# Linear attention feeding an MLP: attention matmuls on 64-column tiles, and the last token block in column pieces

## Chip, cores, metric

The kernel runs on one core of a Trainium2 chip (trn2). The metric is the device time of one execution in microseconds. A ratio is the mean time of one kernel's fast runs over that of the other's in the same rounds, so it is not quite the ratio of the medians that are quoted beside it.

## The reference

Blocked linear attention with decay (4 sequences, 8 heads, 768 positions, head size 64), then an MLP of 512 -> 2048 -> 512 with a sigmoid-approximated GELU over all 3072 tokens. Cut to what matters:

```python
for b in range(nb):                                    # blocks of 64 positions
    intra = (qb @ kb.T * Dmask) @ vb
    inter = (qb * lam_pow) @ kv_state
    out[:, :, sl] = intra + inter
    kv_state = lam_block * kv_state + (kb * rev_pow).T @ vb
...
h = x @ w_in                                           # x: [3072, 512]
return (h * sigmoid(1.702 * h)) @ w_out
```

## The kernel before

The kernel works on six token blocks of 512 tokens. The first two are "double blocks" (256 positions of two sequences, written with `d_...`); the other four are "single blocks" (128 positions of four sequences, `n_...`). Each attention part is slipped in between the MLP matmuls of the token block before it. Two heads share the 128 partitions as a pair `r` or `p`. For the matmul that gives `v.T @ scores` the weights are 128 columns wide, one head's 64 columns of `v` beside 64 zero columns: each head's matmul then adds zeros to the other head's half. The state matmul takes both heads' `k` columns against both heads' `v` columns, and only the two diagonal quarters of its result are used.

```python
v_sb = [const.tile([P, B, NP, 3, D], bf16, ...) for i in range(2)]     # v of head 0 | zeros | v of head 1

def d_state(w, c):                                     # state of a double block
    ...
    for r in range(NP):
        for a in range(2):
            nc.tensor.matmul(one[:, r, :], ks[A, a, r*P:(r+1)*P], vt[A, 2*c+a, r, 0:3:2, :], ...)
    ...                                                # the same with all 128 rows into `two`
def n_state(w, p):                                     # state of a single block, head pair p
    for b in range(B):
        nc.tensor.matmul(ps_kv[:, b, :], cast[...,"k"][:, b%2, p*P:(p+1)*P], v_sb[w%2][:, b, p, 0:3:2, :], ...)
    ...
def n_out(w, p):                                       # output of a single block, head pair p
    for b in range(B):
        nc.tensor.matmul(ps_o[:, b, :], kv[:, b, p, :], qT[:, (b%2)*NP + p, :], start=True, stop=False)
        for h in range(2):
            nc.tensor.matmul(ps_o[:, b, :], vt[:, b, p, h:h+2, :]..., masked[w, p, h][:, b, :], ...)
    ...
# the order in which single-block parts are slipped in; t counts groups of four MLP matmuls
side += [(t, (n_two, x, 0)), (t + 2, (n_two, x, 1))]                    # scores and masks
if x + 1 < NW:
    side += [(t + 2*p + 1, (n_state, x, p)) for p in range(NP)]
side += [(t + 4.5 + 2*p, (n_out, x, p)) for p in range(NP)]
```

The end of the program is the last group of 128 tokens: 16 matmuls into a 128x512 accumulator, one copy out of PSUM by VectorE, one store.

Of the kernel before, what the change touches and what calls it, by code (L numbers as in the profile page):

```python
# [24 lines left out]
def kernel(  # L25
# [13 lines left out]
    nc = tc.nc  # L39
    f32 = mybir.dt.float32  # L40
    bf16 = mybir.dt.bfloat16
    B, H, S, D = q.shape
    P = 128
    NP = H // 2
    W = 512
    ND = 2
    G = W // P
    d_model = H * D
# [9 lines left out]
    MUL = mybir.AluOpType.mult  # L58
    ADD = mybir.AluOpType.add

    NW = S // P

    const = ctx.enter_context(tc.tile_pool(name="const", bufs=1))
# [4 lines left out]
    op = ctx.enter_context(tc.tile_pool(name="op", bufs=4))  # L68
    ps = ctx.enter_context(tc.tile_pool(name="ps", bufs=1, space=bass.MemoryType.PSUM))
# [35 lines left out]
    A, Z = slice(0, 64), slice(64, P)  # L105
# [45 lines left out]
    mk_pow(blk_pow, 1.0 * P)  # L151
    warm = const.tile([P, 1], f32)

    v_sb = [const.tile([P, B, NP, 3, D], bf16, name=f"v_sb{i}") for i in range(2)]
    kv_sb = [const.tile([P, B, NP, P], bf16, name=f"kv{i}") for i in range(2)]

    CW = 4
    NCH = FFC // CW
    w_in_sb = [const.tile([P, KC, CW * P], bf16, name=f"w_in{j}") for j in range(NCH)]
    w_out_sb = [const.tile([P, CW, d_model], bf16, name=f"w_out{j}") for j in range(NCH)]  # L160
# [12 lines left out]
    cast, trans, masked, xT, g_of, h_ps, o_ps, t_ps = {}, {}, {}, {}, {}, {}, {}, {}  # L173

    def acc(name, dt=f32, shape=None):
        return ps.tile(shape or [P, 4, P], dt, tag="a", bufs=5, name=name)
# [15 lines left out]
    def cast_v(w, c):  # L192
        f = loaded.pop((w, c, "v"))
        dst = v_sb[w % 2]
        if w < ND:
            for a in range(2):
                nc.gpsimd.tensor_copy(dst[:, 2 * c + a, :, 0:3:2, :],  # L197
                                      f.rearrange("p (r e) (a d) -> p r e a d", e=2, a=2)[:, :, :, a, :])
        else:
            nc.gpsimd.tensor_copy(dst[:, 2 * c : 2 * c + 2, :, 0:3:2, :].rearrange("p b r e d -> p (b r) e d"),  # L200
                                  f.rearrange("p h (a d) -> p h a d", a=2))

    def turn_pe(w, c, nm):
        x = cast[w, c, nm]
# [34 lines left out]

    def d_state(w, c):  # L240
        ks, vt, b = cast[w, c, "k"], v_sb[w % 2], 2 * w + c
        one, two = acc("ps_kv"), acc("ps_kv")
        for r in range(NP):
            for a in range(2):
                nc.tensor.matmul(one[:, r, :], ks[A, a, r * P : (r + 1) * P], vt[A, 2 * c + a, r, 0:3:2, :],  # L245
                                 start=(a == 0), stop=(a == 1))
        for r in range(NP):
            for a in range(2):
                nc.tensor.matmul(two[:, r, :], ks[:, a, r * P : (r + 1) * P], vt[:, 2 * c + a, r, 0:3:2, :],
                                 start=(a == 0), stop=(a == 1))  # L250
        for i, t in ((1, one), (0, two)):
            for hs in (A, Z):
                nc.scalar.copy(kv_sb[i][hs, b, :, hs], t[hs, :, hs])  # L253

    def d_out(w, c):
        qT, vt, b = trans[w, c, "q"].rearrange("p (r t) s -> p r (t s)", r=NP), v_sb[w % 2], 2 * w + c
        oa, oz = acc("ps_o"), acc("ps_o")
        for r in range(NP):
            nc.tensor.matmul(oz[:, r, :], kv_sb[1][:, b, r, :], qT[:, r, P:], start=(r == 0), stop=False,
                             skip_group_check=True)  # L260
        for r in range(NP):
            for a in range(2):
                for h in range(2):
                    for t, bs in ((oa, A), (oz, Z)):
                        nc.tensor.matmul(t[:, r, :], vt[bs, 2 * c + a, r, h : h + 2, :].rearrange("p e d -> p (e d)"),  # L265
                                         masked[w, c, r // 2, h][bs, r % 2, a, :],
                                         start=(t is oa and r + a + h == 0), stop=(a + h == 2), skip_group_check=True)
        if w not in xT:
            xT[w] = xp.tile([P, NP, W], bf16, tag="x", name="xT")
        for i, t in ((0, oa), (1, oz)):  # L270
            n0 = (2 * c + i) * P
            nc.scalar.copy(xT[w][:, :, n0 : n0 + P], t)  # L272
# [21 lines left out]
                f(w, p)  # L294

    def n_state(w, p):
        ps_kv = acc("ps_kv")
        for b in range(B):
            nc.tensor.matmul(ps_kv[:, b, :], cast[w, b // 2, "k"][:, b % 2, p * P : (p + 1) * P],  # L299
                             v_sb[w % 2][:, b, p, 0:3:2, :], start=True, stop=True)  # L300
        new, old = kv_sb[(w + 1) % 2], kv_sb[w % 2]
        for h, hs in enumerate((A, Z)):
            nc.vector.scalar_tensor_tensor(new[hs, :, p, hs], old[hs, :, p, hs],  # L303
                                           blk_pow[hs, 2 * p + h : 2 * p + h + 1],
                                           ps_kv[hs, :, hs], op0=MUL, op1=ADD)

    def n_out(w, p):
        vt, kv = v_sb[w % 2], kv_sb[w % 2]
        ps_o = acc("ps_o")
        for b in range(B):  # L310
            qT = trans[w, b // 2, "q"]
            nc.tensor.matmul(ps_o[:, b, :], kv[:, b, p, :], qT[:, (b % 2) * NP + p, :], start=True, stop=False)  # L312
            for h in range(2):
                nc.tensor.matmul(ps_o[:, b, :], vt[:, b, p, h : h + 2, :].rearrange("p e d -> p (e d)"),  # L314
                                 masked[w, p, h][:, b, :], start=False, stop=(h == 1))
        if w not in xT:
            xT[w] = xp.tile([P, NP, W], bf16, tag="x", name="xT")
        nc.scalar.copy(xT[w][:, p, :], ps_o.rearrange("p b s -> p (b s)"))  # L318
# [11 lines left out]
        if h_ps[fc][1] == KC * W:  # L330
            nc.scalar.activation(g_of[w][:, fc, :], h_ps.pop(fc)[0], GELU)  # L331

    def mlp2(w, g, j):
        if j == 0:
            o_ps[w, g] = ps.tile([P, d_model], f32, tag="mm", bufs=3, name="ps_out")
        ps_out = o_ps[w, g]
        for fc in range(j * CW, (j + 1) * CW):
            nc.tensor.matmul(ps_out, g_of[w][:, fc, g * P : (g + 1) * P], w_out_sb[j][:, fc % CW, :],  # L338
                             start=(fc == 0), stop=(fc == FFC - 1))
        if j == NCH - 1:  # L340
            o = op.tile([P, d_model], f32, tag="o", name="o_sb")
            nc.vector.tensor_copy(o, ps_out)  # L342
            r0 = (2 * w + g // 2) * S + (g % 2) * P if w < ND else g * S + w * P
            nc.sync.dma_start(out=out[r0 : r0 + P, :], in_=o)

    EARLY = 3
    ALL = slice(0, W)
# [2 lines left out]
    def mlp_items(w):  # L350
        if w < ND:
            parts = [(full, slice(0, W // 2)), (full, slice(W // 2, W))]
        else:
            parts = [(full[:-1], ALL), (full[-1:], ALL)]
        first = [(mlp1, w, fc, kcs, cols) for kcs, cols in parts for fc in range(EARLY)]
        second = [(mlp1, w, fc, full, ALL) for fc in range(EARLY, FFC)]
        if w == 0:
            third = [(mlp2, w, g, j) for j in range(NCH) for g in range(2)]
            third += [(mlp2, w, g, j) for g in range(2, G) for j in range(NCH)]
        else:  # L360
            third = [(mlp2, w, g, j) for g in range(G) for j in range(NCH)]
        return first + second + third

    def gate_pool(x):
# [4 lines left out]

    with tc.manual_schedule():  # L370
        u32 = mybir.dt.uint32
        nc.vector.memset(v_sb[0][:, :, :, 1, :].bitcast(u32), 0)
        for x in kv_sb:
            nc.vector.memset(x.rearrange("p b r s -> p (b r s)").bitcast(u32), 0)
        nc.vector.memset(v_sb[1][:, :, :, 1, :].bitcast(u32), 0)
        nc.scalar.activation(warm, sd_pow[:, 0:1], GELU)

        do_cast(0, 0, "k", nc.vector)
        do_cast(0, 0, "q", nc.vector)
        cast_v(0, 0)  # L380
        do_cast(0, 1, "k", nc.gpsimd)
        gate_pool(loaded[0, 1, "q"][0:1, 0, 0:1])
# [6 lines left out]
        turn_pe(0, 1, "k")  # L389
        turn_pe(0, 1, "q")  # L390
        d_state(0, 0)
        d_out(0, 0)
        cast_v(0, 1)
        for j in range(1, NCH):
            load_w_in(j)
# [4 lines left out]
        d_scores(0, 1, 0)  # L400
        d_scores(0, 1, 1)
        d_state(0, 1)

        side, main = [(EARLY, (d_out, 0, 1))], []
        for w in range(NW):
            n = len(main)
            main += mlp_items(w)
            e = len(main)
            x = w + 1
            if x < ND:  # L410
                for c in range(HF):
                    t = e - 12 + 6 * c
# [5 lines left out]
            elif x < NW:  # L418
# [4 lines left out]
                t = n + 16  # L423
# [42 lines left out]
```

## Time and profile before

| | |
|---|---|
| time | 228.92 us median of 3 runs |
| span of the profiled execution | 226.8 us |
| TensorE (PE) busy | 205.9 us, 91% |
| MLP matmuls' share of the chain that ended last | 35% + 34% |

The page of the kernel before, cut: busy time and share of each engine; busy tenths in 40 slices; the chain of waits that ended last, by engine and then by line.

```profile
PE 205.9 (91%) x1536; PEld 110.6 (49%) x1560; DVE 92.6 (41%) x139; ACT 89.1 (39%) x157; POOL 24.6 (11%) x44
PE   0379799988999999999999999999999999999992
...
PE 82%; ACT 5%; DVE 4%; issue 3%; DMA 3%; SPq 0%; DVEq 0%
PE ps_out L338 35%; PE ps_h L327 34%; PE ps_o L314 3%; DMA qf<-in_q_dram 3%; PE ps_o L265 2%; DVE sm L287 2%; ACT xT L272 2%; ACT qT L213 2%; PE ps_o L312 2%; PE ps_s L280 1%; PE ps_t L208 1%; ACT g_sb L331 1%; DVE qs L183 1%; PE ps_s L231 1%; PE ps_kv L299 1%
```

TensorE is the limit from about 28 us, the sixth slice, on, so what counts is when it *starts* its next matmul. Its busy time is of little use for that, because matmuls overlap. The groups view names the attention matmuls (line, weights' rows*columns, moving shape, count, then busy us and mean ns of one):

```profile
L314 PE MATMUL ps_o<-sm,v_sb 128*128 128x128 bf16 x128 | 12.4, 219 | 0.0
L312 PE MATMUL ps_o<-qT,kv 128*128 128x128 bf16 x64 | 11.5, 219 | 0.0
L265 PE MATMUL ps_o<-sm,v_sb 64*128 64x128 bf16 x128 | 5.0, 238 | 0.0
L299 PE MATMUL ps_kv<-v_sb,ks 128*128 128x128 bf16 x48 | 4.6, 219 | 0.0
```

Each takes 219 to 238 ns from start to modelled end, but the timeline shows how often they start. Its columns are start in us, length of the merged piece, engine, line, operation and shapes, count. Two stretches of the third single block: a state part alone, and an output part followed by a state part.

```profile
108.79 0.39 PE L299 MATMUL ps_kv<-v_sb,ks 128*128 128x128 bf16 x4
109.02 1.03 PE L327 MATMUL ps_h<-xT,w_in 128*128 128x512 bf16 x4
109.98 0.45 PE L280 MATMUL ps_s<-qT,kT 64*128 64x128 bf16 x9
110.58 0.38 PE L280 MATMUL ps_s<-qT,kT 64*128 64x128 bf16 x7 [0.15 <-DVE sm L287]
110.89 1.04 PE L327 MATMUL ps_h<-xT,w_in 128*128 128x512 bf16 x4
...
113.71 0.22 PE L312 MATMUL ps_o<-qT,kv 128*128 128x128 bf16 x1
...
114.38 0.39 PE L299 MATMUL ps_kv<-v_sb,ks 128*128 128x128 bf16 x4
```

The next start is the thing to read: four state matmuls hold TensorE from 108.79 to 109.02, 56 ns each, and twelve output matmuls from 113.71 to 114.38, again 56 ns each.

### The profile page before, as it was taken

What the parts mean: (1) busy time and instruction counts of PE and PEld (TensorE: products, weight loads), DVE (VectorE), ACT (ScalarE), POOL (GpSimd) and SP (SyncE); (2) the same over time, 40 slices, a digit from 0 to 9 for tenths busy, and PEclk for the clock granted to TensorE, in tenths of its full rate; (3) what the DMA queues carried; (4) which work ended last, traced back from release to release, by engine and by line L of the source; (5) the groups of instructions that cost most, each with busy time, mean ns of one, the idle gap of its engine ahead of it and who ended that gap; (6) DMA issues with size and microseconds to landing.
All of it is one profiled execution on the core that took longest, in us unless ns stands there. A gap on an engine that the chain in (4) does not pass through costs nothing.

```text
span 226.8 us, 3726 instructions
## 1 busy us (share of the span) xinstructions
PE 205.9 (91%) x1536; PEld 110.6 (49%) x1560; DVE 92.6 (41%) x139; ACT 89.1 (39%) x157; POOL 24.6 (11%) x44
## 2 busy tenths in 40 slices
PE   0379799988999999999999999999999999999992
PEld 0257644545664465444465444565444564444440
DVE  4473200484780881280971371961452712100121
ACT  5635567246267422056322066322076321276000
POOL 4297000220120003000003000003000000000000
PEclk9999999999999999999999999999999999999998
DMA  5989999999999993169993189991292011200121
GB/s 144 291 169 206 198 200 267 289 248 213 244 242 203 206 225 99 46 141 201 206 227 110 47 172 200 222 219 68 77 155 51 0 49 60 79 0 3 46 80 59
DMA packets 86756, 33.79 MB, mean 149 GB/s; under 512 B 67284, under 2 KB 83668, under 8 KB 86740
## 3 DMA queue, kind: packets, MB, share of 16 engines
q1 hardware_dynamic: 82516, 29.37, 58.8%
q0 software_dynamic: 4224, 4.19, 11.5%
q8 instruction: 12, 0.20, 0.4%
q14 instruction: 4, 0.03, 0.0%
HBM read 27.27 MB, written 6.29 MB: 148 GB/s over the span
## 4 chain that ended last, share of the span: by engine, by line
PE 82%; ACT 5%; DVE 4%; issue 3%; DMA 3%; SPq 0%; DVEq 0%
PE ps_out L338 35%; PE ps_h L327 34%; PE ps_o L314 3%; DMA qf<-in_q_dram 3%; PE ps_o L265 2%; DVE sm L287 2%; ACT xT L272 2%; ACT qT L213 2%; PE ps_o L312 2%; PE ps_s L280 1%; PE ps_t L208 1%; ACT g_sb L331 1%; DVE qs L183 1%; PE ps_s L231 1%; PE ps_kv L299 1%
## 5 line engine op out<-in xcount | busy, mean ns | idle before, releaser
L327 PE MATMUL ps_h<-xT,w_in 128*128 128x512 bf16 (+1 forms) x397 | 86.2, 366 | 2.9 <-ACT xT L272 1.3
L338 PE MATMUL ps_out<-w_out,g_sb 128*128 128x512 bf16 x371 | 86.3, 379 | 0.9 <-issue 0.3
L331 ACT ACTIVATE g_sb<-ps_h 128x512 bf16<-128x512 f32 x96 | 56.0, 597 | 62.3 <-PE ps_h L327 61.8
L327 PEld LDWEIGHTS <-w_in 128*128 128x128 bf16 x408 | 39.0, 98 | 44.3 <-issue 3.6
L338 PEld LDWEIGHTS <-g_sb 128*128 128x128 bf16 x384 | 36.2, 98 | 38.8
L342 DVE COPY o_sb<-ps_out 128x512 f32<-128x512 f32 x24 | 16.6, 691 | 72.9 <-PE ps_out L338 72.9
L287 DVE SCALAR_TENSOR_TENSOR sm<-ps_s,inv_pow,mask 128x512 bf16<-128x512 f32 x32 | 21.7, 744 | 27.0 <-PE ps_s L280 26.9
L318 ACT CAST xT<-ps_o 128x512 bf16<-128x512 f32 x16 | 9.4, 586 | 30.9 <-PE ps_o L314 30.9
L200 POOL CAST v_sb<-vf 128x1024 bf16<-128x1024 f32 x8 | 9.0, 1123 | 96.6 <-DMA vf<-in_v_dram 96.6
L237 DVE SCALAR_TENSOR_TENSOR sm<-ps_s,sd_pow,mask_d 128x256 bf16<-128x256 f32 x32 | 13.1, 478 | 9.4 <-PE ps_s L231 9.4
L314 PE MATMUL ps_o<-sm,v_sb 128*128 128x128 bf16 x128 | 12.4, 219 | 0.0
L303 DVE SCALAR_TENSOR_TENSOR kv<-kv,blk_pow,ps_kv 64x256 bf16<-64x256 bf16 x24 | 11.5, 478 | 1.1 <-PE ps_kv L299 0.6
L312 PE MATMUL ps_o<-qT,kv 128*128 128x128 bf16 x64 | 11.5, 219 | 0.0
L183 DVE TENSOR_TENSOR ks<-kf,kd_pow 128x1024 bf16<-128x1024 f32 x3 | 3.7, 1223 | 17.6 <-DMA kf<-in_k_dram 16.0
L314 PEld LDWEIGHTS <-v_sb 128*128 128x128 bf16 x128 | 9.8, 98 | 1.9
L187 DVE TENSOR_TENSOR ks<-kf,k_pow 128x1024 bf16<-128x1024 f32 x8 | 10.7, 1336 | 0.1
L208 PE MATMUL ps_t<-ident,ks 128*128 128x128 bf16 x32 | 3.3, 265 | 7.9 <-DVE ks L183 7.1
L187 DVE TENSOR_TENSOR qs<-qf,q_pow 128x1024 bf16<-128x1024 f32 x8 | 9.7, 1218 | 0.0
L253 ACT CAST kv<-ps_kv 64x256 bf16<-64x256 f32 x16 | 5.9, 366 | 7.6 <-PE ps_kv L245 7.4
L197 POOL CAST v_sb<-vf 128x512 bf16<-128x512 f32 x8 | 4.8, 617 | 33.1 <-DMA vf<-in_v_dram 33.1
L211 ACT COPY kT<-ps_t 128x1024 bf16<-128x1024 bf16 x4 | 4.1, 1016 | 8.1 <-PE ps_t L208 8.1
L312 PEld LDWEIGHTS <-kv 128*128 128x128 bf16 x64 | 6.3, 98 | 1.9
(54 smaller groups left out, 88.5 us busy)
## 6 DMA issues: line engine op xcount, KB each, us to landing
kf<-in_k_dram SPq DMA_DIRECT2D x12, 512.0 KB, 6.8
qf<-in_q_dram SPq DMA_DIRECT2D x12, 512.0 KB, 7.5
vf<-in_v_dram SPq DMA_DIRECT2D x12, 512.0 KB, 7.3
out_dram<-o_sb SPq DMA_DIRECT2D x24, 256.0 KB, 2.0
w_in<-in_moe_w_in_dram POOLq DMA_DIRECT2D x4, 512.0 KB, 7.0
w_out<-in_moe_w_out_dram POOLq DMA_DIRECT2D x4, 512.0 KB, 15.0
kT<-ks SPq DMA_TRANSPOSE x8, 3.3
qT<-qs SPq DMA_TRANSPOSE x8, 3.3
```

The costliest lines, as they stand in the source:

```text
L187: eng.tensor_tensor(x.rearrange("p b (h d) -> p b h d", h=H), f.rearrange("p (b h) (a d) -> p b (h a) d", b=2, a=2), pw.unsqueeze(3).to_br ...
L200: nc.gpsimd.tensor_copy(dst[:, 2 * c : 2 * c + 2, :, 0:3:2, :].rearrange("p b r e d -> p (b r) e d"), f.rearrange("p h (a d) -> p h a d", ...
L237: nc.vector.scalar_tensor_tensor(sm[:, i], s2[h][:, i], sd_pow[:, hd : hd + 1], mask_d, op0=MUL, op1=MUL)
L287: nc.vector.scalar_tensor_tensor(sm, s, inv_pow[:, 2 * p + h : 2 * p + h + 1], mask.to_broadcast([P, B, P]), op0=MUL, op1=MUL)
L303: nc.vector.scalar_tensor_tensor(new[hs, :, p, hs], old[hs, :, p, hs], blk_pow[hs, 2 * p + h : 2 * p + h + 1], ps_kv[hs, :, hs], op0=MUL, ...
L312: nc.tensor.matmul(ps_o[:, b, :], kv[:, b, p, :], qT[:, (b % 2) * NP + p, :], start=True, stop=False)
L314: nc.tensor.matmul(ps_o[:, b, :], vt[:, b, p, h : h + 2, :].rearrange("p e d -> p (e d)"), masked[w, p, h][:, b, :], start=False, stop=(h ...
L318: nc.scalar.copy(xT[w][:, p, :], ps_o.rearrange("p b s -> p (b s)"))
L327: nc.tensor.matmul(h_ps[fc][0][:, cols], w_in_sb[j][:, kc, i * P : (i + 1) * P], xT[w][:, kc, cols], start=(kc == 0), stop=(kc == KC - 1))
L331: nc.scalar.activation(g_of[w][:, fc, :], h_ps.pop(fc)[0], GELU)
L338: nc.tensor.matmul(ps_out, g_of[w][:, fc, g * P : (g + 1) * P], w_out_sb[j][:, fc % CW, :], start=(fc == 0), stop=(fc == FFC - 1))
L342: nc.vector.tensor_copy(o, ps_out)
```

## The change

The intent: give each head of a pair its own 64 columns of the array. Its weights are then 64 columns wide, its result goes to its own 64 partitions, and two heads can run at the same time; the zero padding of `v` and the unused quarters of the state go away. How a matmul divides the array (rows*columns: 128*128, 128*64, 64*128 or 64*64) is called its mode below, and the time from the start of one matmul, or of one group that starts together, to the next is called a round. Separately, the last 128 tokens are computed in pieces of 256, 128 and 128 columns, so that the final copy and store are small. The diff, cut to its core:

```diff
-    v_sb = [const.tile([P, B, NP, 3, D], bf16, name=f"v_sb{i}") for i in range(2)]
+    v_sb = [const.tile([P, B, H, D], bf16, name=f"v_sb{i}") for i in range(2)]
 ...                                                   # d_state, d_out: the same idea on 64-row tiles too
     def n_state(w, p):
         for b in range(B):
-            nc.tensor.matmul(ps_kv[:, b, :], cast[w, b // 2, "k"][:, b % 2, p * P : (p + 1) * P],
-                             v_sb[w % 2][:, b, p, 0:3:2, :], start=True, stop=True)
+            for h, hs in enumerate((A, Z)):
+                n0 = p * P + h * D
+                nc.tensor.matmul(ps_kv[hs, b, :], cast[w, b // 2, "k"][:, b % 2, n0 : n0 + D],
+                                 v_sb[w % 2][:, b, 2 * p + h, :], start=True, stop=True)
     def n_out(w, p):
-            nc.tensor.matmul(ps_o[:, b, :], kv[:, b, p, :], qT[...], start=True, stop=False)
-            for h in range(2):
-                nc.tensor.matmul(ps_o[:, b, :], vt[:, b, p, h : h + 2, :].rearrange("p e d -> p (e d)"), ...)
+            for hs in (A, Z):
+                nc.tensor.matmul(ps_o[hs, b, :], kv[:, b, p, hs], qT[...], start=(b == 0), stop=False, ...)
+            for h, hs in enumerate((A, Z)):
+                nc.tensor.matmul(ps_o[hs, b, :], vt[:, b, 2 * p + h, :], masked[w, p, h][:, b, :], ...)
 ...
+        if w == NW - 1:
+            third = third[:-NCH]
+            for c0, c1 in ((0, 256), (256, 384), (384, 512)):
+                third += [(mlp2, w, G - 1, j, c0, c1) for j in range(NCH)]
 ...
-        nc.vector.memset(v_sb[0][:, :, :, 1, :].bitcast(u32), 0)      # and v_sb[1]
```

More of the change, by code (lines that the diff above doesn't have):

```diff
@@ L196, in cast_v @@
             for a in range(2):
-                nc.gpsimd.tensor_copy(dst[:, 2 * c + a, :, 0:3:2, :],
-                                      f.rearrange("p (r e) (a d) -> p r e a d", e=2, a=2)[:, :, :, a, :])
-        else:
-            nc.gpsimd.tensor_copy(dst[:, 2 * c : 2 * c + 2, :, 0:3:2, :].rearrange("p b r e d -> p (b r) e d"),
-                                  f.rearrange("p h (a d) -> p h a d", a=2))
+                nc.gpsimd.tensor_copy(dst[:, 2 * c + a], f.rearrange("p h (a d) -> p h a d", a=2)[:, :, a, :])
+        else:
+            nc.gpsimd.tensor_copy(dst[:, 2 * c : 2 * c + 2].rearrange("p b h d -> p (b h d)"),
+                                  f.rearrange("p h e -> p (h e)"))
     def turn_pe(w, c, nm):
@@ L241, in d_state @@
         ks, vt, b = cast[w, c, "k"], v_sb[w % 2], 2 * w + c
-        one, two = acc("ps_kv"), acc("ps_kv")
-        for r in range(NP):
-            for a in range(2):
-                nc.tensor.matmul(one[:, r, :], ks[A, a, r * P : (r + 1) * P], vt[A, 2 * c + a, r, 0:3:2, :],
-                                 start=(a == 0), stop=(a == 1))
-        for r in range(NP):
-            for a in range(2):
-                nc.tensor.matmul(two[:, r, :], ks[:, a, r * P : (r + 1) * P], vt[:, 2 * c + a, r, 0:3:2, :],
-                                 start=(a == 0), stop=(a == 1))
+        one, two = acc("ps_kv", shape=[P, NP, D]), acc("ps_kv", shape=[P, NP, D])
+        for t, rows in ((one, A), (two, slice(0, P))):
+            for r in range(NP):
+                for a in range(2):
+                    for h, hs in enumerate((A, Z)):
+                        n0 = r * P + h * D
+                        nc.tensor.matmul(t[hs, r, :], ks[rows, a, n0 : n0 + D], vt[rows, 2 * c + a, 2 * r + h, :],
+                                         start=(a == 0), stop=(a == 1))
         for i, t in ((1, one), (0, two)):
             for hs in (A, Z):
-                nc.scalar.copy(kv_sb[i][hs, b, :, hs], t[hs, :, hs])
+                nc.scalar.copy(kv_sb[i][hs, b, :, hs], t[hs, :, :])
     def d_out(w, c):
@@ L258, in d_out @@
         for r in range(NP):
-            nc.tensor.matmul(oz[:, r, :], kv_sb[1][:, b, r, :], qT[:, r, P:], start=(r == 0), stop=False,
-                             skip_group_check=True)
+            for hs in (A, Z):
+                nc.tensor.matmul(oz[hs, r, :], kv_sb[1][:, b, r, hs], qT[:, r, P:], start=(r == 0), stop=False,
+                                 skip_group_check=True)
         for r in range(NP):
             for a in range(2):
-                for h in range(2):
-                    for t, bs in ((oa, A), (oz, Z)):
-                        nc.tensor.matmul(t[:, r, :], vt[bs, 2 * c + a, r, h : h + 2, :].rearrange("p e d -> p (e d)"),
+                for t, bs in ((oa, A), (oz, Z)):
+                    for h, hs in enumerate((A, Z)):
+                        nc.tensor.matmul(t[hs, r, :], vt[bs, 2 * c + a, 2 * r + h, :],
                                          masked[w, c, r // 2, h][bs, r % 2, a, :],
-                                         start=(t is oa and r + a + h == 0), stop=(a + h == 2), skip_group_check=True)
+                                         start=(t is oa and r + a == 0), stop=(a == 1), skip_group_check=True)
         if w not in xT:
@@ L296, in n_state @@
     def n_state(w, p):
-        ps_kv = acc("ps_kv")
+        ps_kv = acc("ps_kv", shape=[P, B, D])
         for b in range(B):
-            nc.tensor.matmul(ps_kv[:, b, :], cast[w, b // 2, "k"][:, b % 2, p * P : (p + 1) * P],
-                             v_sb[w % 2][:, b, p, 0:3:2, :], start=True, stop=True)
+            for h, hs in enumerate((A, Z)):
+                n0 = p * P + h * D
+                nc.tensor.matmul(ps_kv[hs, b, :], cast[w, b // 2, "k"][:, b % 2, n0 : n0 + D],
+                                 v_sb[w % 2][:, b, 2 * p + h, :], start=True, stop=True)
         new, old = kv_sb[(w + 1) % 2], kv_sb[w % 2]
@@ L304, in n_state @@
                                            blk_pow[hs, 2 * p + h : 2 * p + h + 1],
-                                           ps_kv[hs, :, hs], op0=MUL, op1=ADD)
+                                           ps_kv[hs], op0=MUL, op1=ADD)
     def n_out(w, p):
@@ L311, in n_out @@
             qT = trans[w, b // 2, "q"]
-            nc.tensor.matmul(ps_o[:, b, :], kv[:, b, p, :], qT[:, (b % 2) * NP + p, :], start=True, stop=False)
-            for h in range(2):
-                nc.tensor.matmul(ps_o[:, b, :], vt[:, b, p, h : h + 2, :].rearrange("p e d -> p (e d)"),
-                                 masked[w, p, h][:, b, :], start=False, stop=(h == 1))
+            for hs in (A, Z):
+                nc.tensor.matmul(ps_o[hs, b, :], kv[:, b, p, hs], qT[:, (b % 2) * NP + p, :], start=(b == 0), stop=False,
+                                 skip_group_check=True)
+            for h, hs in enumerate((A, Z)):
+                nc.tensor.matmul(ps_o[hs, b, :], vt[:, b, 2 * p + h, :], masked[w, p, h][:, b, :],
+                                 start=False, stop=True, skip_group_check=True)
         if w not in xT:
@@ L331, in mlp1, with mlp2 @@
             nc.scalar.activation(g_of[w][:, fc, :], h_ps.pop(fc)[0], GELU)
-    def mlp2(w, g, j):
+    def mlp2(w, g, j, c0=0, c1=None):
+        c1 = c1 or d_model
         if j == 0:
-            o_ps[w, g] = ps.tile([P, d_model], f32, tag="mm", bufs=3, name="ps_out")
-        ps_out = o_ps[w, g]
+            o_ps[w, g, c0] = ps.tile([P, c1 - c0], f32, tag="mm", bufs=3, name="ps_out")
+        ps_out = o_ps[w, g, c0]
         for fc in range(j * CW, (j + 1) * CW):
-            nc.tensor.matmul(ps_out, g_of[w][:, fc, g * P : (g + 1) * P], w_out_sb[j][:, fc % CW, :],
+            nc.tensor.matmul(ps_out, g_of[w][:, fc, g * P : (g + 1) * P], w_out_sb[j][:, fc % CW, c0:c1],
                              start=(fc == 0), stop=(fc == FFC - 1))
         if j == NCH - 1:
-            o = op.tile([P, d_model], f32, tag="o", name="o_sb")
+            o = op.tile([P, d_model], f32, tag="o", name="o_sb")[:, 0 : c1 - c0]
             nc.vector.tensor_copy(o, ps_out)
             r0 = (2 * w + g // 2) * S + (g % 2) * P if w < ND else g * S + w * P
-            nc.sync.dma_start(out=out[r0 : r0 + P, :], in_=o)
+            nc.sync.dma_start(out=out[r0 : r0 + P, c0:c1], in_=o)
     EARLY = 3
@@ L371 @@
         u32 = mybir.dt.uint32
-        nc.vector.memset(v_sb[0][:, :, :, 1, :].bitcast(u32), 0)
         for x in kv_sb:
             nc.vector.memset(x.rearrange("p b r s -> p (b r s)").bitcast(u32), 0)
-        nc.vector.memset(v_sb[1][:, :, :, 1, :].bitcast(u32), 0)
         nc.scalar.activation(warm, sd_pow[:, 0:1], GELU)
```

## The prediction

> **What bounds the kernel now.** TensorE. The page gives PE busy 205.9 of 226.8 us; the chain that ended last is 82% PE, 69% in the two MLP lines, which stay. PE's waits add up to 15 us, nearly all in the first 20 us. From 28 us on PE starts a 512-column matmul every 216 ns. So PE time saved in the attention part should come off the total, except where loads bind (DMA share 9 up to about 60 us).
>
> **What the start times of single matmuls show.** A 128-column matmul costs a round of 56 ns. On 64x128 tiles two start 3 ns apart and share a round (output of the double blocks); on 64x64 tiles (their scores) four do. So disjoint 64-column tiles should too, as the Trainium skill says ("TensorEngine Tiling (Array Packing)", Key Properties: tiles execute independently). It also says there that changing the tiling mode drains TensorE. The trace agrees: 148 to 152 ns instead of 56, about 10 more on the next start: some 105 ns per change. At 64x64 the second set of weight loads starts 28 ns after the first, so I estimate that 64-column rounds can run at 28 ns.
>
> **Savings, estimated from those.**
> - Double blocks, output: 16 rounds become 8, -445 ns, one mode change more, +105. Three times: -1.0 us. The first runs at half clock (107 ns rounds): -0.85.
> - Double blocks, state: 16 rounds of 56 become 16 of 28, -450; one more change in two of them. Three times: -1.1 us. The first hides behind ScalarE's qT copy: 0.
> - Single blocks, output: 12 rounds of 56 become 8, four times, -0.89 us a block; state: 4 rounds of 56 become 4 of 28, four times, -0.44. Before, neither changes the mode. After, each run of them between MLP matmuls changes it twice (210 ns): 5 runs a block (output p is followed directly by state p+1), 4 in the last: +1.05. Net -0.28, thrice, and -0.05 in the last: -0.9 us. Most of the gain is given back here.
> - Tail: the last copy falls from 128x512 (691 ns) to 128x128, estimated 0.29 us; the last store from 256 to 64 KB (2.0 us to landing), estimated -0.5; three passes, +0.1. Together -0.8 us.
> - Zero memsets of v (2 x 485 ns, VectorE) precede the first loads' landing: 0. v casts: off the chain.
>
> Sum -4.6 us. I take off 0.5: (a) PE runs at half clock until 20.1 us; less work in the head may delay the full clock (about 1.2 us, one chance in three); (b) up to 60 us the queue of loads and transposes does not move earlier, so some gain may turn into waits.
>
> **Prediction: 224.8 us**, 8 in 10 between 222.9 and 226.9. Faster by over 2%: 0.38; within 2%: 0.60; slower by over 2%: 0.02.
>
> **What would show it right.** Starts in pairs 3 ns apart at the single blocks' output, in fours at the double blocks' output (32 matmuls in 0.45 us, not 0.9); 28 ns rounds in both state parts; gaps of 150 ns at both ends of each attention run; a last copy near 0.3 us, and 0.7 to 0.9 us less from the last matmul to the end. MLP matmuls stay at 216 ns.
>
> **What would make it wrong.** Column tiles of 128 rows not sharing rounds (16 instead of 12 in the single blocks: slower); 64-column rounds floored at 56 ns (2.5 us less gained); a mode change dearer or cheaper than 105 ns (about 40 more of them: 50 ns each is 2 us); the clock granted later; a new DMA wait before 75 us.

## More of the kernel before

The head and the tail, from the timeline:

```profile
22.51 1.47 PE L327 MATMUL ps_h<-xT,w_in 128*128 128x256 bf16 x12
23.82 0.39 PE L259 MATMUL ps_o<-qT,kv 128*128 128x128 bf16 x4
...
222.50 0.69 DVE L342 COPY o_sb<-ps_out 128x512 f32<-128x512 f32 x1 [2.76 <-PE ps_out L338]
223.22 0.33 SPq L344 DMA_DIRECT2D out_dram<-o_sb  x1
```

## The result

The changed kernel took 226.01 us (median of 4 runs, 225.58 to 226.12) against 228.84 us (4 runs); ratio 0.9878, 95% interval 0.9854 to 0.9901. A second set of 6 runs on another chip gave 226.27 us and 0.9880. So 2.8 us came off, where the prediction had 4.1 us after its allowance and 4.6 us before it. Executions over 1.5% slower than the fastest of the same kernel are left out of the means.

The page after, cut to busy times and the chain by engine:

```profile
PE 206.0 (92%) x1784; PEld 104.9 (47%) x1784; DVE 93.0 (41%) x139; ACT 89.1 (40%) x157; POOL 25.9 (12%) x44
...
PE 88%; ACT 5%; DMA 3%; DVE 2%; issue 1%; SPq 0%; DVEq 0%
```

The groups view after (the line numbers moved: the double blocks' output is now L258 and L264, the single blocks' output L314 and L317, their state L300, the MLP L330 and L342):

```profile
L314 PE MATMUL ps_o<-qT,kv 128*64 128x128 bf16 x128 | 9.3, 225 | 0.0
L317 PE MATMUL ps_o<-sm,v_sb 128*64 128x128 bf16 x128 | 8.9, 219 | 0.0
L300 PE MATMUL ps_kv<-v_sb,ks 128*64 128x64 bf16 x96 | 3.6, 198 | 0.0
L264 PE MATMUL ps_o<-sm,v_sb 64*64 64x128 bf16 x128 | 3.0, 242 | 0.0
```

PE busy stayed at 206 us although the span fell; as said above, it tells nothing. The timeline of the same two stretches of the third single block:

```profile
107.46 0.32 PE L300 MATMUL ps_kv<-v_sb,ks 128*64 128x64 bf16 x8
107.71 1.04 PE L330 MATMUL ps_h<-xT,w_in 128*128 128x512 bf16 x4
108.68 0.85 PE L279 MATMUL ps_s<-qT,kT 64*128 64x128 bf16 x16
109.47 1.04 PE L330 MATMUL ps_h<-xT,w_in 128*128 128x512 bf16 x4
...
112.51 0.25 PE L314 MATMUL ps_o<-qT,kv 128*64 128x128 bf16 x2
112.59 0.22 PE L317 MATMUL ps_o<-sm,v_sb 128*64 128x128 bf16 x2
...
112.98 0.29 PE L300 MATMUL ps_kv<-v_sb,ks 128*64 128x64 bf16 x8
113.20 1.04 PE L342 MATMUL ps_out<-w_out,g_sb 128*128 128x512 bf16 x4
```

The start times of single matmuls, taken from the trace of the first single block, show the mechanism at work:

```
us       ns since the start before it in the trace
78.965   216   MLP, 128x128 weights
79.274   309   output, columns 0-63      (93 ns more than an MLP round: mode change)
79.278     4   output, columns 64-127
79.354    76   next pair, 80 ns after the first one (24 ns more than a round)
79.410    52   next pair, and so on: two matmuls per 56 ns
79.745    52   state, first pair
79.774    25   next pair
79.805    28   next pair, and so on: two matmuls per 31 to 32 ns
79.969   129   MLP again, 132 ns after the last pair (101 ns more than such a round: mode change)
80.194   225   MLP                       (9 ns more)
```

Pairs start 3 to 4 ns apart. Rounds of 64 columns take 31 to 32 ns from pair to pair: the 28 ns of the forecast are what lies between the second matmul of a pair and the first of the next. A change of mode costs 117 ns going in and 110 coming out, some 0.23 us for each run of attention matmuls. The head and the tail after, from the timeline:

```profile
21.91 2.14 PE L330 MATMUL ps_h<-xT,w_in 128*128 128x256 bf16 x12
23.98 0.41 PE L258 MATMUL ps_o<-qT,kv 128*64 128x128 bf16 x8
...
220.17 0.29 DVE L346 COPY o_sb<-ps_out 128x128 f32<-128x128 f32 x1 [0.47 <-PE ps_out L342]
221.06 0.29 DVE L346 COPY o_sb<-ps_out 128x128 f32<-128x128 f32 x1 [0.60 <-PE ps_out L342]
```

In the head the changed kernel reached the first MLP matmuls 0.6 us sooner (21.91 against 22.51), but then took 2.07 us for twelve of them where the kernel before took 1.31, and was behind at the next part (23.98 against 23.82). The starts say why: the matmuls still ran at the half clock, 107 ns per 128 columns, until 23.3 us; in the kernel before that ended at 20.1 us.

The ledger, from the start times in the two traces (a mark is the first MLP matmul after the named part):

| stretch | before us | after us | difference | predicted |
|---|---|---|---|---|
| start to the MLP after both parts of the first double block | 26.37 | 26.12 | -0.25 | -1.64 |
| to the MLP after the second double block | 36.44 | 35.32 | -1.12 | -1.38 |
| four single blocks, to the first MLP half of the last token block | 131.45 | 131.30 | -0.15 | -0.89 |
| to the start of the last copy | 28.24 | 28.32 | +0.08 | +0.1 |
| last copy | 0.69 | 0.29 | -0.40 | -0.40 |
| last store, from its issue to the wait that it released | 2.02 | 1.58 | -0.45 | -0.5 |
| rest (semaphores and drains at the end) | 1.53 | 1.24 | -0.29 | 0 |

Copy and store are separated by some 0.03 us in both. Two terms fell short: the head by 1.4 us and the single blocks by 0.7 us.

### The profile page after: what moved, and what is told of

Same layout as the page of the kernel before. It is cut to its first block, busy times and chain, and to the rows that moved or that the text cites. A ratio compares the mean times of both kernels' runs of the same rounds, so it can differ in the third digit from the quotient of the medians.

```text
span 224.2 us, 4203 instructions
## 1 busy us (share of the span) xinstructions
PE 206.0 (92%) x1784; PEld 104.9 (47%) x1784; DVE 93.0 (41%) x139; ACT 89.1 (40%) x157; POOL 25.9 (12%) x44
## 4 chain that ended last, share of the span: by engine, by line
PE 88%; ACT 5%; DMA 3%; DVE 2%; issue 1%; SPq 0%; DVEq 0%
PE ps_h L330 37%; PE ps_out L342 37%; DMA qf<-in_q_dram 3%; PE ps_o L314 2%; PE ps_s L279 2%; ACT qT L212 2%; ACT xT L271 2%; PE ps_kv L247 2%; PE ps_o L317 2%; PE ps_t L207 1%; PE ps_o L264 1%; PE ps_s L230 1%; ACT g_sb L334 1%; DVE qs L183 1%; PE ps_kv L300 1%; PE ps_o L258 1%
## 5 line engine op out<-in xcount | busy, mean ns | idle before, releaser
L330 PE MATMUL ps_h<-xT,w_in 128*128 128x512 bf16 (+1 forms) x408 | 87.6, 369 | 2.4 <-ACT xT L271 1.3
L342 PE MATMUL ps_out<-w_out,g_sb 128*128 128x512 bf16 (+2 forms) x416 | 88.4, 363 | 0.0
L330 PEld LDWEIGHTS <-w_in 128*128 128x128 bf16 x408 | 39.1, 98 | 44.9 <-issue 3.6
L342 PEld LDWEIGHTS <-g_sb 128*128 128x128 bf16 x416 | 37.2, 98 | 38.8
L346 DVE COPY o_sb<-ps_out 128x512 f32<-128x512 f32 (+2 forms) x26 | 16.9, 650 | 71.5 <-PE ps_out L342 71.5
L199 POOL CAST v_sb<-vf 128x1024 bf16<-128x1024 f32 x8 | 10.4, 1294 | 92.5 <-DMA vf<-in_v_dram 92.5
L187 DVE TENSOR_TENSOR qs<-qf,q_pow 128x1024 bf16<-128x1024 f32 x8 | 10.6, 1323 | 0.0
L314 PEld LDWEIGHTS <-kv 128*64 128x64 bf16 x128 | 6.7, 109 | 6.8 <-issue 6.8
L314 PE MATMUL ps_o<-qT,kv 128*64 128x128 bf16 x128 | 9.3, 225 | 0.0
L317 PE MATMUL ps_o<-sm,v_sb 128*64 128x128 bf16 x128 | 8.9, 219 | 0.0
L317 PEld LDWEIGHTS <-v_sb 128*64 128x64 bf16 x128 | 7.2, 110 | 0.0
```

The source lines that it names most:

```text
L187: eng.tensor_tensor(x.rearrange("p b (h d) -> p b h d", h=H), f.rearrange("p (b h) (a d) -> p b (h a) d", b=2, a=2), pw.unsqueeze(3).to_br ...
L199: nc.gpsimd.tensor_copy(dst[:, 2 * c : 2 * c + 2].rearrange("p b h d -> p (b h d)"), f.rearrange("p h e -> p (h e)"))
L314: nc.tensor.matmul(ps_o[hs, b, :], kv[:, b, p, hs], qT[:, (b % 2) * NP + p, :], start=(b == 0), stop=False, skip_group_check=True)
L317: nc.tensor.matmul(ps_o[hs, b, :], vt[:, b, 2 * p + h, :], masked[w, p, h][:, b, :], start=False, stop=True, skip_group_check=True)
L330: nc.tensor.matmul(h_ps[fc][0][:, cols], w_in_sb[j][:, kc, i * P : (i + 1) * P], xT[w][:, kc, cols], start=(kc == 0), stop=(kc == KC - 1))
L342: nc.tensor.matmul(ps_out, g_of[w][:, fc, g * P : (g + 1) * P], w_out_sb[j][:, fc % CW, c0:c1], start=(fc == 0), stop=(fc == FFC - 1))
```

## The experiments

My theory: (1) in the head, the gain was eaten because the full clock came later, and it came later because TensorE had less to do; (2) in the single blocks the matmuls got as fast as foreseen, or nearly (the state's rounds), but I had miscounted the runs: there are 6 per block and not 5, as the first two state parts stand alone, and each pays two mode changes. Rivals: the clock comes at random moments whatever the work; and the single blocks lost their gain to some other limit. All runs gave correct results.

### 1. Parts by themselves, and a filler in the head

The filler adds eight idle matmuls where TensorE waits for ScalarE anyway:

```diff
+    def fill(x, n, cols):
+        t = ps.tile([P, W], f32, tag="mm", bufs=3, name="ps_fill")
+        for _ in range(n):
+            nc.tensor.matmul(t[:, 0:cols], x[:, 0:P], x[:, P : P + cols], start=True, stop=True)
 ...
         d_state(0, 0)
+        fill(cast[0, 0, "k"][:, 0, :], 8, P)
         d_out(0, 0)
```

> The changed kernel plus 8 idle 128x128 matmuls (results unused) in the gap between the first double block's state and output, where TensorE waits 0.7 us for ScalarE anyway. In the changed kernel's trace the full clock came at 23.3 us instead of 20.1 and the work lost some 1.4 us there. Theory (the clock is granted one step later because the head holds less TensorE work): the filler brings the grant back to about 20 us and the time falls by 1.0 to 1.5 us below the changed kernel (226.0), to 224.5 to 225.0. Rival (the grant falls at random within a step, whatever the work): no systematic change, 226.0 within 0.4, or a time that scatters by 1.5 us between runs.

Measured: 224.97 us, ratio 0.9847 (0.9834 to 0.9859), against 0.9878 and 0.9880 of the changed kernel without it, which is 0.7 us of the 228.5 us of the kernel before (the medians differ by 1.0). The full clock came at 20.9 us. Its timeline of the head:

```profile
21.57 1.48 PE L330 MATMUL ps_h<-xT,w_in 128*128 128x256 bf16 x12
22.98 0.41 PE L258 MATMUL ps_o<-qT,kv 128*64 128x128 bf16 x8
```

Adding work made the kernel faster: the twelve MLP matmuls are back at 1.41 us from their first start to the next part (1.31 before the change, plus the change of mode that now follows them), and that part starts 1.0 us sooner than in the changed kernel. This supports theory (1). The intervals of the two ratios just touch (0.9854 to 0.9901 without the filler); the single runs lie apart (225.23 us at most with it, 225.58 at least without), though not all were on the same chip.

The other three runs put one part of the change into the kernel before. The double-block and single-block versions keep the padded `v` and take the head's columns out of it (index `2 * h` of the middle axis).

```diff
 # tail only: the mlp2 and mlp_items lines of the diff above, nothing else
 # double only: d_state and d_out of the diff above, with vt[rows, 2*c+a, r, 2*h, :]
 # single only: n_state and n_out of the diff above, with v_sb[w%2][:, b, p, 2*h, :]
```

> The kernel before with nothing but the last token block in three column pieces. Traces of before and after: from the last matmul to the landing of the last store 0.8 us less. Expected 228.8 - 0.8 = 228.0 (227.7 to 228.3). Rival (the tail's gain is hidden by the stores or by the end of the program): within 0.2 of before.

Measured: 227.86 us, ratio 0.9967 (0.9954 to 0.9979): 0.75 us. As expected.

> The kernel before with only the double blocks' state and output on 64-column tiles (v still padded, old tail, old single blocks). Theory: the clock comes late (about 23.3 us) as in the changed kernel, so the head gains only 0.25 us; the second double block gains 1.1: 228.8 - 1.4 = 227.4 (227.0 to 227.8). Rival (late clock not due to this part): clock at 20.1 us and 228.8 - 2.8 = 226.0.

Measured: 227.47 us, ratio 0.9957 (0.9941 to 0.9973): 1.0 us, with runs from 226.84 to 228.10. The full clock came at 24.1 us, so the late clock belongs to the double-block part. The second double block took 35.32 us in its stretch of the ledger, as in the changed kernel.

> The kernel before with only the single blocks' state and output on 64-column tiles. Theory (6 runs per block between MLP matmuls, not 5, so mode changes give back nearly all): 228.8 - 0.2 = 228.6 (228.3 to 228.8), full clock at 20.1 us as before. Rival (my forecast of 5 runs was right and the gain was lost to something else in the changed kernel): 228.8 - 0.9 = 227.9.

Measured: 228.50 us, ratio 1.0002 (0.9990 to 1.0014). The single-block part of the change, on its own, is worth nothing that can be told from zero; the full clock came at 20.6 us. The forecast of 0.9 us is ruled out.

The three ratios multiply to 0.9926, while the whole change has 0.988. In the profiled runs the difference lies in the head. The mark at 26.37 us of the kernel before came at 26.65 with the tail part and at 26.60 with the single part, neither of which touches the head, and the double part's came at 26.53 against 26.12 of the changed kernel: 0.28 + 0.23 + 0.41 = 0.9 us in all. I take that for the scatter of the head from one execution to the next (the head's mark came between 25.84 and 26.77 us in the four traces with the whole changed head and no filler), so the parts' sum should not be read finer than this. An effect of the unpadded `v`, which no part had, is not excluded.

### 2. Fewer runs of attention matmuls, and an early clock

The yardstick on the same chip:

> The changed kernel unaltered, as the yardstick of the next three on the same chip, and a second trace of its head. Theory: the full clock comes after 22 us again (steps of 3.4 us whose phase differs from run to run), 226.0 within 0.5. Rival (the grant is a matter of chance alone): as likely near 20 us as near 23.

Measured: 226.27 us, ratio 0.9880 (0.9841 to 0.9920); full clock at 22.8 us.

To test the price of the runs, the same matmuls are put into fewer runs:

```diff
-                if x + 1 < NW:
-                    side += [(t + 2 * p + 1, (n_state, x, p)) for p in range(NP)]
-                side += [(t + 4.5 + 2 * p, (n_out, x, p)) for p in range(NP)]
+                for p in range(NP):
+                    tt = t + 4.5 + 2 * p                 # 4 runs; for 2 runs: t + 6.5 + 4 * (p // 2)
+                    side += [(tt, (n_out, x, p))]
+                    if x + 1 < NW:
+                        side += [(tt, (n_state, x, p))]
```

> The changed kernel with each single block's state p issued right after its output p, so that there are 4 runs of attention matmuls between MLP matmuls in a block instead of 6; same matmuls. Theory (each run costs two mode changes, about 0.22 us): three blocks lose two runs each, -1.3 us against the changed kernel. Rival (single blocks limited by something other than mode changes): within 0.3 of the changed kernel.

Measured: 224.31 us, ratio 0.9797 (0.9759 to 0.9835): 2.0 us below the changed kernel.

> The same, but two outputs and two states per run: 2 runs a block instead of 6, in the last block 2 instead of 4. Theory: 3*4 + 2 = 14 runs fewer, -3.1 us against the changed kernel, less if ScalarE's or VectorE's evacuations now make TensorE wait. Rival: within 0.3 of the changed kernel, or slower.

Measured: 222.53 us, ratio 0.9712 (0.9668 to 0.9755): 3.7 us below the changed kernel. Its timeline, where the state and output matmuls now run on without a return to the full array:

```profile
112.82 0.25 PE L314 MATMUL ps_o<-qT,kv 128*64 128x128 bf16 x2
...
113.29 0.29 PE L300 MATMUL ps_kv<-v_sb,ks 128*64 128x64 bf16 x8
113.41 0.23 PE L314 MATMUL ps_o<-qT,kv 128*64 128x128 bf16 x2
...
114.08 1.25 PE L342 MATMUL ps_out<-w_out,g_sb 128*128 128x512 bf16 x5
```

Inside the run a state part now takes 0.12 us (113.29 to 113.41) where it took 0.22 before the change, and the run as a whole returns to the MLP at 114.08 after 1.27 us. Both regroupings gained 0.5 to 0.6 us more than their mode changes. The timelines show where: the second scores of a block held TensorE for 0.91 us in the kernel before (109.98 to 110.89) and 0.79 in the changed one (108.68 to 109.47). In both regrouped kernels they take 0.55 us like the first scores, as no state part stands between the two any more. That is 0.23 us in each of three blocks. With it the sums close: 6 runs x 0.23 + 0.7 = 2.1 us, and 14 x 0.23 + 0.7 = 3.9 us; in the traces the stretch from the end of the second double block to the end of the program is 2.08 and 3.87 us shorter than in the changed kernel. I take the cause of the 0.23 us to be the state's accumulator, which uses one of the five PSUM buffers that the scores need; no run separates this from the load on VectorE.

> The changed kernel plus 11 idle 512-column matmuls on a zeroed tile while TensorE waits for the first load (2 to 7 us). Theory (work on TensorE, whatever it computes, brings the full clock): granted before about 11 us, and the head shorter by the 1.4 us that the late grant cost and by up to 1 us more: 223.5 to 224.8. Rival (matmuls of zeros don't count, or the clock falls back before 20 us because the head is too thin): 226.0 within 0.4.

```diff
+        fill(kv_sb[0].rearrange("p b r s -> p (b r s)"), 11, W)      # zeros, before the first load lands
         do_cast(0, 0, "k", nc.vector)
```

Measured: 225.77 us, ratio 0.9858 (0.9819 to 0.9897), 0.5 us below the changed kernel and not clear of noise: a miss. Its table of stretches shows a part of why (after the stretch and its length: busy us and count of PE, PEld, DVE, ACT and POOL, then the granted clock, DMA share and GB/s):

```profile
7.00:11.00 4.00, 1.35 (x24) 1.11 (x28) 1.24 (x2) 2.48 (x3) 1.41 (x3) 1.00 1.21 290
11.00:14.00 3.00, 1.31 (x40) 1.14 (x37) 2.54 (x5) 0.00 (x0) 2.74 (x2) 0.65 1.11 265
14.00:17.00 3.00, 2.46 (x44) 1.82 (x41) 1.82 (x5) 2.61 (x4) 3.00 (x5) 0.50 0.32 30
20.00:24.00 4.00, 4.00 (x95) 3.10 (x86) 2.69 (x7) 1.56 (x5) 1.47 (x2) 0.73 1.22 198
```

Zeros do bring the clock, at 5.1 us; but with TensorE idle most of the time from 7 us on it is taken back at 11.9 us and comes again only at 22.2. That is not all: the head's mark still came at 25.26 us, 0.6 to 0.9 us sooner than in the two traces of the changed kernel, but the next stretch of the ledger took 35.95 us instead of 35.32, as the load of the second double block's `k` landed at 41.0 us instead of 39.7. Part 3 shows what had delayed it.

The distances of the three clock events are 6.83 and 10.24 us, which are 2 and 3 times 3.41 us. That is the window of the Trainium skill's "TensorE: Matmul & The Clock Gate" (Part 1: a free-running window of 3413 ns). In all 14 traces the last stretch at full clock is a whole number of it too, from 58 to 64 windows (in the kernel before 204.80 us, 60 windows). The grants by head:

| head of the kernel | full clock at, us |
|---|---|
| as before (before, tail only, single only) | 20.1, 21.9, 20.6 |
| as changed (changed, again, double only, 4 runs, 2 runs) | 23.3, 22.8, 24.1, 24.1, 24.6 |
| changed + 8 fillers (first run, last run below) | 20.9, 20.9 |

The changed heads without filler stand apart: their earliest grant (22.8) comes after the latest of the other two groups (21.9), which do overlap. So the work decides in which window the grant can come, and the phase of the window scatters it by up to 1.8 us. Both theory and rival had a part of it, but the shift by the change is systematic.

### 3. The clock up all through the head, and the combinations

Here the waits of the head are filled too, with 5, 5, 6, 4 and 4 matmuls of 512 columns:

```diff
         turn_pe(0, 0, "k")
+        fill(cast[0, 0, "k"][:, 0, :], 5, W)
         turn_pe(0, 0, "q")
+        fill(cast[0, 0, "k"][:, 0, :], 5, W)
 ...                                        # 6 and 4 around turn_pe(0, 1, "k"), 4 before d_out(0, 0)
```

> The changed kernel with idle matmuls (results unused) before the first load lands and in every longer wait of TensorE up to the first double block's output. The previous run showed that the early filler alone brings the full clock at 5.1 us, that it is taken back at 11.9 and comes again at 22.2. Theory: with the waits filled too the clock stays up from about 5 us; head shorter by 1.5 to 2.5 us: 226.1 - 2 = 224.1 (223.5 to 224.8). Rival (what the head waits for is loads and VectorE and ScalarE, so the clock hardly matters; or the fillers delay real work): 225.5 or more.

Measured: 226.00 us, ratio 0.9890 (0.9877 to 0.9903): the rival's number, and a miss for me. The clock did what I wanted: up at 7.5 us and not taken back, and the head's mark came at 23.67 us instead of 26.12. But the next mark, after the second double block, came at 61.51 us against 61.44. One line of VectorE's timeline of this run (in brackets the idle time before it, and what ended it):

```profile
41.24 1.23 DVE L183 TENSOR_TENSOR ks<-kf,kd_pow 128x1024 bf16<-128x1024 f32 x1 [19.54 <-DMA kf<-in_k_dram]
```

TensorE reached the transposes of the second double block early and, by the waits view, waited 1.8 us for its `k`, whose load landed at 41.2 us. In the changed kernel the load landed at 39.7 us, `k` was ready 1.2 us later, and TensorE came to that point at 42.97, without a wait. So there are some 2 us of slack there. But most of the wait is not the price of a shorter head, as the load itself came some 1.6 us later. The fillers had moved it: the weight load that stands in line ahead of it was issued at 14.29 us instead of 13.27, because the GpSimd copy that gates it took 1.17 us instead of 0.18. The timelines of VectorE and GpSimd in this run:

```profile
13.09 1.22 DVE L183 TENSOR_TENSOR qs<-qf,qd_pow 128x1024 bf16<-128x1024 f32 x1
13.18 1.17 POOL L378 COPY behind_q<-qf 1x1 f32<-1x1 f32 x1
```

VectorE's multiply of `q` started sooner here (13.09 us; 13.67 in the changed kernel), so that it was running when the copy started, and the copy ended 0.04 us after it. The same holds in the two other traces with a long copy (1.18 us), the early filler above and the run of both findings below. In the other eleven VectorE started the multiply after the copy's start, and the copy took 0.18 us. No run moved the two apart on purpose. With `k` ready at 40.7 to 40.9 us, as in the traces with a short copy on the same chip and in the changed kernel, TensorE would have waited 0.2 to 0.4 us here and not 1.8 (my estimate: its matmul before started at 40.30 us and holds it for 0.22).

> The kernel before with the same idle matmuls, so that both kernels can be compared with the clock up from 5 us. Theory: the change is then worth its full size, as nothing is lost to a later grant: this kernel 3.0 to 3.4 us above the changed kernel with fillers (2.3 to 2.8 without fillers), so about 227.3. Rival (the clock is not what ate the head's gain): the same distance as without fillers, 2.5, or less.

Measured: 227.73 us, ratio 0.9954 (0.9935 to 0.9974), with runs from 226.67 to 227.99. It lies 1.7 us above the changed kernel with the same fillers, and not 3.0 to 3.4: a miss. But the two traces don't compare like with like. Here the gating copy took 0.18 us, the load landed at 39.5 us and TensorE did not wait for `k`, while the changed kernel did. Up to the head's mark, with the clock up from 8.2 and 7.5 us, the change is worth 1.06 us (24.73 against 23.67), where the first pair of traces had 0.25; at the next mark the changed kernel is 0.34 us behind (61.51 against 61.17). So the first half of the theory, that the late clock ate most of the head's gain, is supported by this pair of traces, and by the next mark the late load had cancelled it. The trace is of one of the two faster runs of this kernel (226.86 us); the four at 227.6 to 228.0 have none.

> Both findings together: two outputs and two states per run in the single blocks, and the fillers. If they add: 222.5 - 2 = 220.5 (219.8 to 221.3). If an earlier head only runs into the loads of the second double block: 222 or more.

Measured: 221.85 us, ratio 0.9708 (0.9696 to 0.9720): equal to two runs per block without fillers by the ratios, 0.7 us below by the medians, so not told apart. The gating copy took 1.18 us here too, the load landed at 40.6 us, and TensorE waited 1.3 us for `k`.

> Two outputs and two states per run, with only the 8 small fillers of the first experiment. If that filler is worth 0.7 to 1.0 us here too: 221.6 (221.2 to 222.0). If its gain there was chance of the phase: 222.5.

Measured: 221.27 us, ratio 0.9692 (0.9665 to 0.9720). This is the fastest version that I found, 3.1% below the kernel before. Its head mark came at 25.13 us and the next at 60.45 us, with no wait for loads. That the small filler adds to the regrouping is likely from this trace (the mark was at 26.77 us without it), but the intervals of the two ratios overlap.

## Why the prediction was right or wrong

The measured 226.0 us lies inside the range and within 2%, the outcome given the highest chance. The middle, 224.8, was 1.2 us too low. Some of the agreement is luck: the -0.29 us of the ledger's last row were not foreseen and made up for a part of what the head and the single blocks lacked.

- **"Disjoint 64-column tiles should too", "64-column rounds can run at 28 ns", mode changes "some 105 ns": right in kind, the last two a little too low.** Pairs start 3 to 4 ns apart, fours in the double blocks (a whole output part of the second one, from its first start to the next MLP matmul, took 0.92 us against 1.32), rounds of 64 columns take 31 to 32 ns, and a mode change costs 110 to 117 ns.
- **Tail, -0.8 us: right.** The trace has -0.77 us up to the landing (+0.08 - 0.40 - 0.45), the run of that part alone 0.75 us.
- **Second double block: -1.38 us foreseen, -1.12 measured.** The changes of mode cost a little more than assumed, and the 32 rounds of 64 columns took 3 to 4 ns more each, some 0.1 us.
- **"5 runs a block (output p is followed directly by state p+1)": wrong, and the largest false step about the kernel itself.** The timeline shows states 0 and 1 alone, states 2 and 3 behind an output, outputs 2 and 3 alone: 6 runs. With measured pieces (each including the entry): a lone state went from 0.22 to 0.35 us, a lone output stayed at 0.67, output with state went from 0.89 to 0.80. Two of each make +0.08 us, the second scores gave back 0.13, and the block gained 0.05 to 0.06 us, as the ledger has it, instead of 0.28. Without the scores the block misses the forecast by 0.36 us: 0.23 are the sixth run, and the rest is the price of a run (0.23 us and not 0.21) and the rounds of 31 to 32 ns. The order was there to be read in the timeline before; I read it off one block's merged chain.
- **Head, -0.85 and -0.79: wrong in its sum, with the cause named.** I gave the late clock one chance in three and took off 0.5 us for it and the loads together. It came in all five traces with the changed head and no filler, and in the first pair of traces the head gained 0.25 us instead of 1.64. With the clock up early in both kernels it gained 1.06, and with the eight fillers 1.24 (25.13 against 26.37); what is missing from 1.64 then was not traced.
- **Hedge (b), the loads: not seen in the changed kernel.** TensorE waited for them in three runs with fillers, but there the load landed 1.0 to 1.6 us later than in the changed kernel, behind the delayed GpSimd copy. A shorter head by itself would have met a wait of 0.2 to 0.4 us (the estimate above).

## What to carry to other kernels

Count tile-mode changes before splitting the array: here two of them cost 0.23 us, as much as the whole state part that they were to speed up, so the split paid only after its matmuls were gathered into long runs. Taking work off TensorE in a thin start-up phase can delay its full clock, and a few idle matmuls in an existing wait can win that back; but before filling everything look at what the other engines then do sooner (here VectorE's multiply, during which the GpSimd copy that gates the loads took six times as long). And read a schedule's order from the timeline of several blocks rather than from one.

## What the Trainium skill lacked or had wrong

- "TensorEngine Tiling (Array Packing)", Key Properties: it says that a change of tiling mode drains TensorE, but not what that costs. Here it was 110 to 117 ns per change at full clock, next to rounds of 31 or 56 ns.
- "TensorE: Matmul & The Clock Gate", Part 1: it gives about 25 ns as the smallest distance of two starts and does not say there that this is for one tile. Between different tiles it was 3 to 4 ns here, which is what the page's own Part 3 gives (about 4 ns); on one tile 64 columns took 31 to 32 ns.
- The same page and part: it does not say how busy a window must be. Here a head with somewhat less work missed the windows ending before 22.8 us in all five traces, while eight more matmuls, about 1 us, brought the grant at 20.9 us in both; and the clock was taken back at 11.9 us with TensorE busy for 1.35 of the 4 us from 7 us on.
- "TensorEngine Tiling (Array Packing)", Restrictions: it says that column tiling turns off the fast weight load, but not what that costs. With 128 moving columns it had no visible price here: the rounds stayed at 56 ns. Whether the 31 to 32 ns with 64 columns hold one, no run tells.
